# A planned attention and soft-MoE kernel: VectorE's slot-softmax steps in smaller parts inside its wait for the row maxima, value products in pieces of four

## The chip, the cores and the metric

The kernel runs on one core of a Trainium2 chip. The metric is the device time of one execution in microseconds. Three runs of the kernel before took 1103.34, 1103.69 and 1103.90 us, median 1103.69 us.

## The reference

An attention over pooled keys is followed by a soft mixture of experts on its output. The shapes are q (4, 12288, 128), kv (4, 384, 32, 128), 32 slots, 8 experts with 1024 hidden features.

```python
kv_pool = kv.reshape(B, H // r, r, W // r, r, C).mean(axis=(2, 4))      # r = 4: 768 keys per batch
k = v = kv_pool.reshape(B, -1, C) @ w_sr
s = scale * (q @ k.transpose(0, 2, 1))
a = softmax(s, axis=-1)                       # less the row maximum, 1e-09 in the denominator
x = (a @ v).reshape(B * N, C)                 # 49152 rows
logits = x @ phi
d = softmax(logits, axis=0)                   # over all 49152 rows, for each slot
slot_out = experts(d.T @ x)                   # relu(slot @ w1) @ w2, four slots per expert
c = softmax(logits, axis=1)                   # over the 32 slots, for each row
return c @ slot_out
```

## The kernel before

The 49152 query rows are worked on in 96 blocks of 512. A block has six score tiles of 128 keys by 512 rows, two to a PSUM tile (`s0`, `s1`, `s2`, one buffer each). To keep float32 accuracy, q and k are split into a high and a low part, so each score tile is three matmuls (L478 to L480), 18 for a block. Then, for a block:

- VectorE takes the maximum over the keys out of each pair of score tiles (L485, three times), folds the three results (L495) and spreads them for a matmul (L497, tile `rq`). TensorE finishes the maximum across the partitions with one matmul by a selection matrix (L505), and VectorE takes its result up (L510) and turns it into a tile as wide as the block (L515, `mb`). In the text this chain is the row-maximum chain, and L505 is its matmul.
- VectorE subtracts `mb` from the scores in four instructions (L523, two wide and two narrow), which also frees the score tiles for the next block's 18 matmuls.
- ScalarE takes the exponential twice for each half of the block, to float16 (`phi`, L530) and to float32 (`t`, L534); GpSimd subtracts one from the other (`plo`, L539), so that `phi` and `plo` together carry the weights accurately.
- TensorE multiplies the weights by the values, two blocks later. For each of four chunks of 128 rows there are twelve matmuls with `phi` (L556, L557, six key tiles by a high and a low part of the values) and six with `plo` (L564). The result `px` lies in one of two PSUM banks (`m0`, `m1`), two chunks to a bank, and ScalarE copies it to `xl` (L574).

Four blocks make a group. For each group the softmax over rows goes on with a running maximum and a running sum, in steps that the code names 0 to 7: reciprocal of the attention's denominator (0r, L611), logits (1l, GpSimd, L628), their maximum (2, L633 and L635), its spread over the partitions (2q, 2h, 2l, and the matmul 3m, L656), the new running maximum (3, L663, L665, L670), difference, exponential and scaling (4, 5e, 5m: GpSimd L675, ScalarE L684, GpSimd L690), the factor for the old sum (6r, L697; 6s on ScalarE), the slot products (7m, L709, 16 matmuls, in an `m` bank) and the addition to the running sum (7a, L715). Apart from that, L720 takes the row maxima of the logits for the last softmax.

For each batch the keys are pooled and projected, the values get a power-of-two scale out of their largest absolute value (L383 to L409); the largest value is spread over the partitions by a float32 matmul of a diagonal tile `dg` with `ones` (L396). After the last block come the experts and the output stage.

The order of the instructions on each engine is made by a planner (`Plan`), which knows for each operation an engine, a cost, a latency, a due number, and which buffers it takes and frees, and plays the program forward, always taking the operation with the lowest due number among those that can start about now. An operation with `hot=True` (the row-maximum chain) goes first if it can start soon, and a piece of other work is put before it only if it ends in time. The engines then run that order as it stands, waiting for semaphores. The plan's own times set only the order.

Of the kernel before, what the change touches and what calls it, by code (L numbers as in the profile page):

```python
# [32 lines left out]

class Plan:
# [13 lines left out]
    def op(self, eng, cost, lat, prio, deps, fn, acq=(), use=(), at=0.0, slack=0.0, hot=False, raw=0.0):  # L48
# [5 lines left out]
        self.ops.append((eng, cost, lat, prio, list(deps), fn, list(acq), at, slack, hot, raw, list(use)))  # L54
        return n

    def emit(self):
# [115 lines left out]
def attention_then_soft_moe(ctx: ExitStack, tc: tile.TileContext, qT, kv0, kvT, w_sr, w_srT, phi, w1, w2, outT):  # L173
# [456 lines left out]
    def g2(g):  # L630
        d = G[g]
        cm = sm2(g, "cm", [P, TG])[:, : nt(g)]
        nc.vector.tensor_reduce(out=cm, in_=d["L"], axis=X, op=ALU.max, apply_transpose=True)  # L633
# [84 lines left out]
    def k_max(g):  # L718
        o, n = GB[g][0] * TB, nt(g)
        nc.vector.tensor_reduce(out=RM[:, o : o + n], in_=LL[:, o : o + n, :], axis=X, op=ALU.max)  # L720
# [103 lines left out]
    def kv_ops(b, base, step, dep0, dep1):  # L824
# [20 lines left out]
        s = op("PE", 0.6, 0.4, base + step * 5.5, d, lambda: kv_s_mm(b), acq=[("m", ("pa", b))])  # L845
# [10 lines left out]
    def group_ops(g):  # L856
# [398 lines left out]
```

## Time and profile before

| | |
|---|---|
| median of three runs | 1103.69 us (1103.34 to 1103.90) |
| profiled execution, own time | 1102.28 us |
| its span | 1100.5 us (1.8 us lie around it) |
| busy share: TensorE, VectorE, ScalarE, GpSimd | 93%, 89%, 75%, 79% |
| TensorE weight loads | 80% |

A span row of the page's second part has 40 slices of 27.5 us. TensorE stands at 8 or 9 tenths in all but the first and the last few; the tail, about the last 100 us, moves the output. In the timeline a row has its start in us from the span's start, its duration, the engine, the line, the tile written and the tiles read, and how many instructions were merged; in brackets is the idle time before it. Matmuls are pipelined: one begins before the one ahead has ended, so the distance of their starts counts and not their durations.

### The profile page before, as it was taken

Reading aid. Unit: us, or ns where it says so; the run is one execution under the profiler, and the core shown is the slowest. Engines: PE = TensorE matmul, PEld = TensorE weight load, DVE = VectorE, ACT = ScalarE, POOL = GpSimd, SP = SyncE. Lnnn points to the kernel's source line nnn. Section 1 sums busy time; section 2 is a strip of 40 time slices with the busy share of each in tenths; the row PEclk is TensorE's granted clock in tenths of the full one; section 3 lists DMA queues with packets and bytes.
Section 4 is the critical chain, followed back from the end, with each engine's and each line's share of the span. In section 5 each row is a group of like instructions: output and inputs, shape, how many; then the busy total and the mean of one; then the engine's idle time right before and its main releaser. Section 6 shows DMA issues by size and latency. Waiting matters only on the chain.

```text
span 1100.5 us, 24542 instructions
## 1 busy us (share of the span) xinstructions
PE 1028.4 (93%) x10102; PEld 879.2 (80%) x10102; DVE 982.6 (89%) x1494; ACT 826.7 (75%) x1029; POOL 871.8 (79%) x503
## 2 busy tenths in 40 slices
PE   3699999999999999999999999999999999997874
PEld 2588888888888888888888888888888888886342
DVE  7899889899889999899999988989989989997895
ACT  1677778778778878878877788788788777875564
POOL 1579898798899989789899989789889889873341
PEclk9899999999999999999999999999999999999887
DMA  9316401111137300120145310120110110113398
GB/s 345 119 30 146 106 15 40 40 58 40 40 59 154 83 28 13 39 80 19 40 99 114 82 40 2 40 96 2 39 40 2 40 40 1 39 40 116 132 418 368
DMA packets 17406, 89.14 MB, mean 81 GB/s; under 512 B 1680, under 2 KB 3984, under 8 KB 11152
## 3 DMA queue, kind: packets, MB, share of 16 engines
q1 hardware_dynamic: 13408, 69.47, 17.5%
q0 software_dynamic: 3312, 17.70, 8.5%
q8 instruction: 80, 1.31, 0.5%
q10 hardware_dynamic: 576, 0.41, 0.1%
q14 instruction: 30, 0.25, 0.1%
HBM read 58.87 MB, written 25.17 MB: 76 GB/s over the span
## 4 chain that ended last, share of the span: by engine, by line
PE 60%; ACT 18%; DVE 16%; POOL 3%; issue 2%; DMA 1%; SPq 0%; DVEq 0%; ACTq 0%
PE m L564 11%; PE m L556 10%; PE m L557 10%; ACT phi L530 8%; PE s L478 8%; PE s L479 7%; PE s L480 7%; ACT t L534 7%; DVE t L523 4%; DVE r L485 3%; PE m L709 2%; DVE o L1149 2%; PE m L505 2%; POOL plo L539 1%; DVE mb L515 1%
## 5 line engine op out<-in xcount | busy, mean ns | idle before, releaser
L539 POOL TENSOR_TENSOR plo<-t,phi 128x1536 f16<-128x1536 f32 x190 | 594.9, 3136 | 122.1 <-ACT t L534 121.4
L530 ACT ACTIVATE phi<-t,lnk 128x1536 f16<-128x1536 f32 x192 | 301.4, 1570 | 113.8 <-DVE t L523 113.5
L485 DVE TRANSPOSE_TENSOR_REDUCE r<-s 128x32 f32<-128x1024 f32 x288 | 348.7, 1234 | 29.4 <-PE s L480 25.7
L556 PE MATMUL m<-vhi,phi 128*128 128x161 f16 x2280 | 354.7, 234 | 3.0 <-DVE m L510 1.5
L557 PE MATMUL m<-vlo,phi 128*128 128x160 f16 x2280 | 353.8, 233 | 0.0
L523 DVE TENSOR_TENSOR t<-s,mb 128x1024 f32<-128x1024 f32 (+1 forms) x384 | 343.0, 951 | 9.6 <-POOL LL L628 0.5
L534 ACT ACTIVATE t<-t,lnk 128x1536 f32<-128x1536 f32 x192 | 301.6, 1571 | 3.3
L478 PE MATMUL s<-qhi,khi 128*128 128x512 f32 x576 | 239.9, 417 | 6.1 <-DVE t L523 5.8
L556 PEld LDWEIGHTS <-phi 128*128 128x128 f16 x2304 | 224.2, 98 | 23.8 <-issue 23.8
L557 PEld LDWEIGHTS <-phi 128*128 128x128 f16 x2304 | 225.1, 98 | 5.0 <-issue 3.4
L564 PE MATMUL m<-vhi,plo 128*128 128x161 f16 x2280 | 227.7, 234 | 0.4 <-POOL plo L539 0.4
L479 PE MATMUL s<-qlo,khi 128*128 128x512 f32 x576 | 226.8, 394 | 0.0
L480 PE MATMUL s<-qhi,klo 128*128 128x512 f32 x576 | 226.6, 393 | 0.0
L564 PEld LDWEIGHTS <-plo 128*128 128x128 f16 x2304 | 169.9, 98 | 1.2 <-POOL plo L539 0.6
L468 POOL TENSOR_TENSOR qlo<-q,qhi 128x512 fp32r<-128x512 f32 x96 | 128.4, 1338 | 25.4 <-ACT qhi L464 25.4
L574 ACT ACTIVATE xl<-m 128x322 f32<-128x322 f32 x189 | 80.9, 428 | 81.4 <-PE m L564 81.2
L478 PEld LDWEIGHTS s<-qhi,khi 128*128 128x128 f32 x576 | 109.1, 189 | 33.1 <-issue 7.3
L480 PEld LDWEIGHTS s<-qhi,klo 128*128 128x128 f32 x576 | 108.9, 189 | 24.8 <-DVE klo L358 0.5
L479 PEld LDWEIGHTS s<-qlo,khi 128*128 128x128 f32 x576 | 109.4, 190 | 18.7 <-issue 0.7
L515 DVE STREAM_TRANSPOSE mb<-m 128x512 f32<-128x512 f32 x96 | 68.3, 712 | 3.3
L464 ACT ACTIVATE qhi<-q 128x512 fp32r<-128x512 f32 x96 | 59.1, 616 | 1.8 <-DMA q<-qT 1.0
L749 POOL TENSOR_TENSOR LL<-LL,RM 128x512 f32<-128x512 f32 (+2 forms) x25 | 24.8, 1013 | 32.6 <-DVE RM L744 32.6
(146 smaller groups left out, 819.1 us busy)
## 6 DMA issues: line engine op xcount, KB each, us to landing
q<-qT SPq DMA_DIRECT2D x23, 1024.0 KB, 5.0
outT<-o SPq DMA_DIRECT2D x21, 1024.0 KB, 6.3
kva<-kvT POOLq DMA_DIRECT2D x9, 1536.0 KB, 10.8
kva<-kvT SPq DMA_DIRECT2D x3, 1536.0 KB, 10.3
kv<-kv SPq DMA_DIRECT2D x8, 512.0 KB, 5.6
w<-w SPq DMA_DIRECT2D x2, 1536.0 KB, 7.0
w<-w SPq DMA_DIRECT2D x4, 768.0 KB, 4.1
outT<-o SPq DMA_DIRECT2D x6, 512.0 KB, 5.7
```

The lines of the kernel that those rows point to most:

```text
L468: nc.gpsimd.tensor_tensor(out=lo, in0=q_src(i), in1=hi.bitcast(F32), op=ALU.subtract)
L478: nc.tensor.matmul(s, khi[:, ks], hi, start=True, stop=False)
L479: nc.tensor.matmul(s, khi[:, ks], lo, start=False, stop=False)
L480: nc.tensor.matmul(s, klo[:, ks], hi, start=False, stop=True)
L485: nc.vector.tensor_reduce(out=MX[i][:, 2 * u : 2 * u + 2, :].rearrange("p t b -> p (t b)"), in_=S[i, u].rearrange("p t (b j) -> p (t b) j" ...
L523: nc.vector.tensor_tensor(out=TT_[i, h][:, o : o + n, :], in0=S[i, t // 2][:, u : u + n, :], in1=MX[i].unsqueeze(1).broadcast_to([P, n, BQ ...
L530: nc.scalar.activation(hi, TT_[i, h], AF.Exp, bias=lnk, scale=SCALE)
L534: nc.scalar.activation(t, t, AF.Exp, bias=lnk, scale=SCALE)
L539: eng.tensor_tensor(out=lo, in0=TT_.pop((i, h)), in1=PP[i, h], op=ALU.subtract)
L556: nc.tensor.matmul(px, p, vhi[:, t, :], start=(t == 0), stop=False)
L557: nc.tensor.matmul(px[:, 1:], p, vlo[:, t, :], start=False, stop=False)
L564: nc.tensor.matmul(px, PP[i, t // TH][1][:, t % TH, ks], vhi[:, t, :], start=False, stop=(t == NT - 1))
```

## The change

Five things are done, some of them only in the planner's numbers.

1. VectorE's steps of a group are cut smaller: the maximum of the logits (L633) becomes two instructions of half the width, the group's row maxima (L720) four instructions of a quarter, and the running maximum becomes an operation of its own, apart from L663 and L665. The arithmetic is the same.
2. The planner gets a kind of operation called `fill`: until a due time it is taken only where it delays no other operation by more than 0.02 us. VectorE's group steps and the row-maximum quarters are of this kind. And between L497 and L510 VectorE takes only operations that end within 0.55 us of the plan's time.
3. The twelve `phi` products of a chunk, so far one operation of the plan, become three of four matmuls, so that the plan can put other work between them.
4. The tiles `dg` and `ones` become bfloat16, and with them the matmul L396.
5. Costs and latencies in the plan are changed (the row-maximum chain, 0r, 3, 6r, 7a), which moves the order but not the work.

```diff
+AVS = 2
+SPARE = 0.02
...
+            if e in limit:
+                found = [f for f in found if ops[f[2]][9] or f[0] + ops[f[2]][1] <= limit[e]]
...
+            spare = [f for f in found if ops[f[2]][12] is not None and f[0] < ops[f[2]][12]]
+            if spare:
+                rest = [f for f in found if f not in spare]
+                first = min(rest)[0] if rest else inf
+                found = rest + [f for f in spare if f[0] + ops[f[2]][1] <= first + SPARE]
...
-    ones = cp.tile([P, P], F32, tag="ones", name="ones")
+    ones = cp.tile([P, P], BF16, tag="ones", name="ones")
...
-                bp.tile([P, 2, P], F32, tag="dg", name=f"dg_{b}", bufs=1),
+                bp.tile([P, 2, P], BF16, tag="dg", name=f"dg_{b}", bufs=1),
...
-        for t in range(NT):
+        for t in range(t0, t0 + AVS):
...
-        go("2", "DVE", dve(n512) + 0.13, [o["1l"]], g2)
+            go("2a", "DVE", dve(n512 // 2) + 0.06, [o["1l"]], lambda g: g2(g, 0, n16 // 2), fill=True)
+            go("2a", "DVE", dve(n512 // 2) + 0.06, [o["2a"]], lambda g: g2(g, n16 // 2, n16), fill=True)
+        go("2", "DVE", 0.17, [o["2a"]], g2c, fill=True)
...
-        r2 = op("DVE", 0.36, 0.08, T0 + 2, ..., hot=True, raw=0.14)
-        pe = op("PE", 0.16, 0.3, T0 - 10, ..., hot=True)
+        r2 = op("DVE", 0.58, 0.06, T0 + 2, ..., hot=True, raw=0.1, gap=GAP)
+        pe = op("PE", 0.12, 0.12, T0 - 10, ..., hot=True)
...
-            a1 = op("PE", 12 * 0.0705, 0.17, p, ..., lambda i=i, k=k: av_hi(i, k), ...)
+            for t in range(0, NT, AVS):
+                a1 = op("PE", 2 * AVS * 0.0702, 0.17, p, ..., lambda i=i, k=k, t=t: av_hi(i, k, t), ...)
...
-        a = op("DVE", dve(n), 0.08, p, [ops["L", g]] + late, lambda g=g: k_max(g))
+            a = [op("DVE", dve(TB * NS) + 0.05, 0.08, p, [ops["L", g]], lambda g=g, u=u: k_max(g, u), fill=p + 3 * PER) for u in range(GB[g][1])]
```

What this makes of the order is shown at three places. In these rows a line number is that of the kernel which the row is from; the change shifts them (L485 becomes L501, L497 L513, L505 L521, L510 L526, L556 and L557 L572 and L573, L564 L580, L709 L732, L720 L745).

First place: VectorE, the maxima of block 35, ahead of which (before) the logits' maximum `cm` of a group stands. Before, ahead of the row maxima `r` and inside the wait between `rq` and the next `m`:

```order
L633 TENSOR_REDUCE cm_4994<-LL 128x16
L635 TENSOR_REDUCE cmt_4996<-cm_4994 128x1
L485 TENSOR_REDUCE r_35_5002<-s_0_4978 128x32
L485 TENSOR_REDUCE r_35_5002<-s_1_4989 128x32
L485 TENSOR_REDUCE r_35_5002<-s_2_5005 128x32
L495 TENSOR_REDUCE m_116<-r_35_5002 128x16
L497 TENSOR_TENSOR rq_5054<-m_116,quad 128x64
L720 TENSOR_REDUCE RM<-LL 128x16
L510 TENSOR_REDUCE m_35_5070<-m_116 128x16
```

Now:

```order
L501 TENSOR_REDUCE r_35_5022<-s_0_5005 128x32
L650 TENSOR_REDUCE cm_5032<-LL 128x8
L501 TENSOR_REDUCE r_35_5022<-s_1_5016 128x32
L650 TENSOR_REDUCE cm_5032<-LL 128x8
L501 TENSOR_REDUCE r_35_5022<-s_2_5028 128x32
L655 TENSOR_REDUCE cmt_5074<-cm_5032 128x1
L511 TENSOR_REDUCE m_117<-r_35_5022 128x16
L513 TENSOR_TENSOR rq_5081<-m_117,quad 128x64
L745 TENSOR_REDUCE RM<-LL 128x4
L526 TENSOR_REDUCE m_35_5095<-m_117 128x16
```

The two halves of `cm` stand between the row maxima, `cmt` behind them, and a quarter of the group's row maxima in the wait, where the whole stood.

Second place: VectorE, block 33, where the factor `al` and the running sum `acc` stand, before and now:

```order
L697 TENSOR_REDUCE al_4713<-da_4567 128x1
L485 TENSOR_REDUCE r_33_4724<-s_0_4689 128x32
L715 TENSOR_TENSOR acc<-acc,m_116 128x129
L485 TENSOR_REDUCE r_33_4724<-s_1_4720 128x32
L485 TENSOR_REDUCE r_33_4724<-s_2_4733 128x32
L495 TENSOR_REDUCE m_116<-r_33_4724 128x16
```

```order
L501 TENSOR_REDUCE r_33_4730<-s_0_4713 128x32
L501 TENSOR_REDUCE r_33_4730<-s_1_4725 128x32
L720 TENSOR_REDUCE al_4765<-da_4654 128x1
L501 TENSOR_REDUCE r_33_4730<-s_2_4737 128x32
L745 TENSOR_REDUCE RM<-LL 128x4 x2
L738 TENSOR_TENSOR acc<-acc,m_117 128x129
L511 TENSOR_REDUCE m_117<-r_33_4730 128x16
```

The factor and the sum have moved behind the second and the third row maximum, with two quarters of the group's row maxima ahead of the sum.

Third place: TensorE in the same block, around the 16 slot products, before (behind the first of the six score tiles) and now (behind the last):

```order
L478 MATMUL s_0_4689<-qhi_4495,khi_2405 128x512
L479 MATMUL s_0_4689<-qlo_4496,khi_2405 128x512
L480 MATMUL s_0_4689<-qhi_4495,klo_2406 128x512
L709 MATMUL m_116<-xl_3802,D_4565 32x129 x16
L478 MATMUL s_0_4689<-qhi_4495,khi_2405 128x512
```

```order
L494 MATMUL s_2_4737<-qhi_4478,khi_2387 128x512
L495 MATMUL s_2_4737<-qlo_4479,khi_2387 128x512
L496 MATMUL s_2_4737<-qhi_4478,klo_2388 128x512
L732 MATMUL m_117<-xl_3812,D_4652 32x129 x16
L572 LDWEIGHTS phi_0_4575
```

The slot products now lie between the score tiles and the value products that lead to the row-maximum matmul. That matmul itself, 30 products later, stands between eight and four `phi` products of a chunk, where it stood behind all twelve.

More of the change, by code (lines that the diff above doesn't have):

```diff
@@ L46, in __init__, with op @@
         self.bank = 0
-    def op(self, eng, cost, lat, prio, deps, fn, acq=(), use=(), at=0.0, slack=0.0, hot=False, raw=0.0):
+    def op(self, eng, cost, lat, prio, deps, fn, acq=(), use=(), at=0.0, slack=0.0, hot=False, raw=0.0, fill=None, gap=0.0):
         n = len(self.ops)
@@ L53, in op @@
             self.users.setdefault(key, []).append(n)
-        self.ops.append((eng, cost, lat, prio, list(deps), fn, list(acq), at, slack, hot, raw, list(use)))
+        self.ops.append((eng, cost, lat, prio, list(deps), fn, list(acq), at, slack, hot, raw, list(use), fill, gap))
         return n
@@ L143, in emit @@
             free[e] = t + cost
+            if ops[n][13] > 0:
+                limit[e] = t + cost + ops[n][13]
+            elif ops[n][13] < 0:
+                limit.pop(e, None)
             end = done[n] = t + cost + lat
@@ L292, in attention_then_soft_moe @@
     SL = 0.5
+    LATE = 6.0
+    GAP = 0.55
     def kv_load(plan_):
@@ L715, in g7a, with k_max @@
         nc.vector.tensor_tensor(out=acc, in0=acc, in1=G[g]["pd"][:, : C + 1], op=ALU.add)
-    def k_max(g):
+    def k_max(g, u=None):
         o, n = GB[g][0] * TB, nt(g)
+        if u is not None:
+            o, n = o + u * TB, TB
         nc.vector.tensor_reduce(out=RM[:, o : o + n], in_=LL[:, o : o + n, :], axis=X, op=ALU.max)
@@ L844, in kv_ops @@
         d = [op("ACT", 0.4, 0.1, base + step * 5, m[0] + m[1], lambda k=k: kv_d(b, k)) for k in range(2)]
[L845 removed]
+        s = op("PE", 0.25, 0.4, base + step * 5.5, d, lambda: kv_s_mm(b), acq=[("m", ("pa", b))])
         s = op("DVE", 1.1, 0.08, base + step * 5.5, [s], lambda: kv_s_g(b), use=[("m", ("pa", b))])
@@ L882, in group_ops, with go @@
         k = [0]
-        def go(name, eng, cost, dep, f, acq=(), use=(), path=None):
+        def go(name, eng, cost, dep, f, acq=(), use=(), path=None, fill=False):
             k[0] += 1
-            o[name] = op(eng, cost, 0.08, base + step * k[0], dep, lambda: f(g), acq=list(acq), use=[xl] + list(use) if name in ("0", "1v", "1l", "7m") else list(use), slack=0.0 if fast else SL, raw=0.14)
+            due = base + step * k[0] + LATE if fill and not fast else None
+            o[name] = op(eng, cost, 0.08, base + step * k[0], dep, lambda: f(g), acq=list(acq), use=[xl] + list(use) if name in ("0", "1v", "1l", "7m") else list(use), slack=0.0 if fast else SL, raw=0.14, fill=due)
         go("0", small, sm_(1), deps, g0)
-        go("0r", "DVE", 0.18, [o["0"]], g0r)
+        go("0r", "DVE", 0.21, [o["0"]], g0r, fill=True)
         go("1u", small, sm_(1), [o["0r"]], g1u)
@@ L900, in group_ops @@
         go("3m", "PE", 0.25 if fast else 0.12, [o["2q"]], g3m, acq=[mc])
-        go("3", "DVE", 0.45, [o["3m"]] + ([ops["g3", g - 1]] if g else []), g3, use=[mc])
+        go("3c", "DVE", 0.42, [o["3m"]], g3, use=[mc], fill=True)
+        go("3", "DVE", 0.19, [o["3c"]] + ([ops["g3", g - 1]] if g else []), g3r, use=[mc], fill=True)
         ops["g3", g] = o["3"]
@@ L907, in group_ops @@
         if g:
-            go("6r", "DVE", 0.1, [o["5m"]], g6r)
+            go("6r", "DVE", 0.18, [o["5m"]], g6r, fill=True)
             go("6s", small, 0.3, [o["6r"]] + prev, g6s)
@@ L911, in group_ops @@
         go("7m", "PE", 0.07 * n16, [o["5m"], o["1v"]], g7m, acq=[md], use=[("D", g)])
-        go("7a", "DVE", 0.21, [o["7m"]] + prev, g7a, use=[md])
+        go("7a", "DVE", 0.25, [o["7m"]] + prev, g7a, use=[md], fill=True)
         ops["g7", g] = o["7a"]
@@ L1025, in attention_then_soft_moe @@
         late = [] if g < FAST - 1 else end_ + [last[LG, "g"]]
-        a = op("DVE", dve(n), 0.08, p, [ops["L", g]] + late, lambda g=g: k_max(g))
-        a = op("POOL", 1.05 * n / 512, 0.1, p, [a, ops["g4", g]], lambda g=g: k_sub(g))
+        if late:
+            a = [op("DVE", dve(n), 0.08, p, [ops["L", g]] + late, lambda g=g: k_max(g))]
+        else:
+            a = [op("DVE", dve(TB * NS) + 0.05, 0.08, p, [ops["L", g]], lambda g=g, u=u: k_max(g, u), fill=p + 3 * PER) for u in range(GB[g][1])]
+        a = op("POOL", 1.05 * n / 512, 0.1, p, a + [ops["g4", g]], lambda g=g: k_sub(g))
         ops["ke", g] = op("ACT", act(n), 0.1, p, [a], lambda g=g: k_exp(g))
```

34 lines of the change are left out of this document (22 added, 12 removed).

## The prediction

> **What bounds the kernel now.** I read the page's busy shares first, then the windows, the list of waits, and the timeline of one group of four blocks.
>
> ```profile
> PE 1028.4 (93%) x10102; PEld 879.2 (80%) x10102; DVE 982.6 (89%) x1494; ACT 826.7 (75%) x1029; POOL 871.8 (79%) x503
> ...
> 130.53:170.52 39.99, 39.45 (x399) 34.64 (x399) 36.53 (x53) 31.69 (x39) 35.53 (x21) 1.00 0.22 55
> 571.50:611.50 40.00, 39.44 (x402) 34.65 (x400) 36.54 (x54) 31.67 (x38) 36.90 (x22) 1.00 0.56 116
> ...
> DVE m L510 <- PE m L505: 30.3, 71, 0.5
> DVE r L485 <- PE s L480: 25.7, 33, 1.0
> PE m L505 <- ACT t L534: 6.6, 14, 0.8
> PEld m L505 <- ACT t L534: 10.2, 17, 1.0
> ```
>
> TensorE is busy 93% of the span and 98.6% of a 40 us stretch in the middle, at the full granted clock (1.00); VectorE is busy 91% there, ScalarE 79%, GpSimd 89%. So two engines are nearly full, and each is seen waiting for the other: VectorE 30.3 us for the row-maximum matmul L505, TensorE 16.8 us ahead of that same matmul. (The list names ScalarE for the latter; `rq`, the input of L505, is VectorE's, and the rows below show L505 starting 0.14 us after `rq`.) What can be gained without taking work off TensorE is its idle time, and that is small. Two stretches 441 us apart have the same length, so one group can stand for the rest. It runs from one L505 to the fourth after it:
>
> ```profile
> 354.93 0.27 PE L505 MATMUL m<-rq,sel_r 128*128 128x64 f32 x1
> 358.01 0.47 PE L478 MATMUL s<-qhi,khi 128*128 128x512 f32 x1
> 358.88 1.09 PE L709 MATMUL m<-xl,D 128*32 128x129 f32 x32
> 359.90 0.50 PE L478 MATMUL s<-qhi,khi 128*128 128x512 f32 x1
> 363.48 0.24 PE L556 MATMUL m<-vhi,phi 128*128 128x161 f16 x1
> 365.61 0.30 PE L505 MATMUL m<-rq,sel_r 128*128 128x64 f32 x1
> 368.72 0.47 PE L478 MATMUL s<-qhi,khi 128*128 128x512 f32 x1
> 372.93 0.24 PE L556 MATMUL m<-vhi,phi 128*128 128x161 f16 x1
> 375.14 0.27 PE L505 MATMUL m<-rq,sel_r 128*128 128x64 f32 x1
> 383.72 0.23 PE L556 MATMUL m<-vhi,phi 128*128 128x161 f16 x1
> 384.48 0.23 PE L557 MATMUL m<-vlo,phi 128*128 128x160 f16 x1
> 385.15 0.27 PE L505 MATMUL m<-rq,sel_r 128*128 128x64 f32 x1 [0.44 <-ACT t L534]
> 394.95 0.27 PE L505 MATMUL m<-rq,sel_r 128*128 128x64 f32 x1
> ```
>
> The four intervals are 10.68 ("sum", with the 16 slot products L709), 9.53 ("reciprocal"), 10.01 ("maximum") and 9.80 us ("new maximum"), together 40.02. TensorE's pieces can be read off: from L505 to the score tiles 3.08 (6, 12, 6, 12, 6 value products), the 18 score matmuls 4.21 (368.72 to 372.93), then 12, 6 and 12 value products 2.13 (363.48 to 365.61, where L505 follows at once), twelve of them 0.84 (383.72 to 384.48 and one more). In the maximum interval it idles 0.6 us: twelve products end at 384.55, L505 starts at 385.15.
>
> VectorE in the same group:
>
> ```profile
> 359.78 0.18 DVE L697 TENSOR_REDUCE al<-da 128x1 f32<-128x32 f32 x1
> 360.92 1.25 DVE L485 TRANSPOSE_TENSOR_REDUCE r<-s 128x32 f32<-128x1024 f32 x1 [0.96 <-PE s L480]
> 365.94 0.23 DVE L510 TENSOR_REDUCE m<-m 128x16 f32<-128x64 f32 x1 [0.39 <-PE m L505]
> 367.02 3.55 DVE L523 TENSOR_TENSOR t<-s,mb 128x1024 f32<-128x1024 f32 x4
> 370.48 2.53 DVE L485 TRANSPOSE_TENSOR_REDUCE r<-s 128x32 f32<-128x1024 f32 x2
> 372.94 0.21 DVE L611 RECIPROCAL r<-xl 128x16 f32<-128x16 f32 x1
> 373.12 1.25 DVE L485 TRANSPOSE_TENSOR_REDUCE r<-s 128x32 f32<-128x1024 f32 x1
> 374.40 0.33 DVE L495 TENSOR_REDUCE m<-r 128x16 f32<-128x96 f32 x1
> 374.77 0.23 DVE L497 TENSOR_TENSOR rq<-m,quad 128x64 fp32r<-128x64 f32 x1
> 379.99 0.70 DVE L633 TRANSPOSE_TENSOR_REDUCE cm<-LL 128x16 f32<-128x512 f32 x1
> 387.72 0.15 DVE L663 TENSOR_REDUCE c<-m 128x1 f32<-128x4 f32 x1
> 388.17 0.19 DVE L670 TENSOR_TENSOR mrun<-mrun,m 128x32 f32<-128x32 f32 x1
> 390.61 3.50 DVE L485 TRANSPOSE_TENSOR_REDUCE r<-s 128x32 f32<-128x1024 f32 x3
> ```
>
> The reciprocal interval shows the loop. The last row maximum starts 0.19 after the score tiles end (372.93 to 373.12), `rq` is ready 1.88 later (375.00), L505 follows 0.14 after that, so L505 comes 2.02 after the last row maximum starts; TensorE, with 2.13 of products to do, is ready 0.09 sooner. Reckoned from an L505, the first row maximum can start at 4.87 (365.61 to 370.48), and each takes 1.16 more (three in 3.50, each overlapping the next by 0.08). In the maximum and new-maximum intervals VectorE's group steps make the row maxima late, and TensorE waits 0.6 and 0.3 (the pieces are 9.42 of the 9.80, and step 3m's two small matmuls); in the sum interval TensorE is late by the slot products, and VectorE waits 0.96.
>
> **The change part by part**, by the new order, as distances from the L505 that opens the interval.
>
> *Maximum interval.* Ahead of the row maxima nothing stands now; two halves of L633 stand between them.
>
> ```profile
> L633 DVE TRANSPOSE_TENSOR_REDUCE cm<-LL x25: 311/702/703, 96.7 to 1011.9; 128x16 f32<-128x512 f32 x23, 128x12 f32<-128x384 f32 x1, 128x4 f32<-128x128 f32 x1
> L720 DVE TENSOR_REDUCE RM<-LL x25: 266/675/686, 100.5 to 1017.4; 128x16 f32<-128x512 f32 x23, 128x12 f32<-128x384 f32 x1, 128x4 f32<-128x128 f32 x1
> L675 POOL TENSOR_TENSOR D<-LL,mrun x23: 1273/1302/1750, 106.3 to 992.8; 128x512 f32<-128x512 f32 x23
> L690 POOL TENSOR_TENSOR D<-D,rv x23: 1042/1048/1065, 110.7 to 997.3; 128x512 f32<-128x512 f32 x23
> L539 POOL TENSOR_TENSOR plo<-t,phi x190: 3099/3118/3577, 39.0 to 994.2; 128x1536 f16<-128x1536 f32 x190
> ...
> 358.17 1.58 ACT L530 ACTIVATE phi<-t,lnk 128x1536 f16<-128x1536 f32 x1 [1.53 <-DVE t L523]
> ...
> L396 PE MATMUL m<-dg,ones x8: 378/379/483, 29.2 to 739.6; 128*128 128x256 f32 x8
> ```
>
> Between 0.311 at 128 elements and 0.702 at 512, a half (256) comes to 0.44, 0.36 net of the overlap. The last row maximum starts at 4.87 + 2 x (1.16 + 0.36) = 7.91, L505 at 9.94 with 2.03. TensorE has six more products ahead of L505 (0.43): 3.08 + 4.21 + 2.13 + 0.43 = 9.85. I take 9.95 (9.85 to 10.1, the upper end if the small L635 behind the third maximum isn't hidden): 0.06 gained, and the six products no longer stand behind L505.
>
> *New-maximum interval.* L663, L665, L670 leave the middle of the subtractions and go between the row maxima: 0.34 (387.72 to 388.14 less the overlap) and 0.11. Last maximum 4.87 + 1.16 + 0.34 + 1.16 + 0.11 = 7.64, L505 at 9.67. TensorE, now 2.66 from its score tiles, has to wait for the first subtraction (1.23 of the 3.55, ending at 2.6) and is ready at 2.7 + 4.21 + 2.13 = 9.1, so it idles about 0.5. Gain 0.13. The quarter of L720 that stands in this interval's and the next one's wait (0.27 by the 0.266 at 128 elements) fits into 0.39, where the whole (0.675) did not.
>
> *Sum interval.* TensorE: 3.08, score tiles 4.21, slot products 1.02 and 0.1 for the switch, then 0.85 + 0.44 and eight products 0.56: 10.26, against 10.68. Of the 0.42, 0.28 are the four products that now follow L505, 0.14 the second switch inside the score tiles. VectorE, with the last maximum at 7.29 + 0.19 = 7.48, two quarters (0.19 each net), the sum 0.21 and L495 to L497 in 0.60, has `rq` at 9.8 and waits: 0.3 of cover. ScalarE's part of the sum now stands behind three exponentials of 1.58 (the first, at 358.17, starts 3.2 after L505), a copy of `px` and one of q, so done at about 9.0: not late.
>
> *Reciprocal interval.* The four products come first: score tiles end at 3.38 + 4.21 = 7.59, L505 at 7.59 + 0.19 + 2.02 = 9.80, 0.27 longer than before.
>
> Sum: 10.26 + 9.80 + 9.95 + 9.67 = 39.68, that is 0.34 less per group. The order has this pattern in 18 of 22 groups. In three, all twelve products and six more stand between the slot products and L505: 10.97 + 9.38 (the score tiles start at 2.7 there) + 9.95 + 9.67 = 39.97, 0.05 less. Six of the 18 hold a batch's key and value work, which TensorE does anyway; I count half for them. So 12 x 0.34 + 6 x 0.17 + 3 x 0.05 = 5.3 us.
>
> *L396 in bfloat16*: four uses, three in the loop, each with two records of 0.38. A bfloat16 matmul of this width is not in the trace: between nothing and 0.7 saved each. I take the middle, 1.0 us for three. *Start and tail*: the first seven blocks keep their order; in the tail the last groups' steps shuffle, and TensorE's slot products of the last full group go behind more value products. Bounds -2 to +2, taken as 0. DMA issues stay in their order on SP; GpSimd's keep their number.
>
> Together -6.3 us: the profiled execution's 1102.28 becomes 1096.0, and against the median, 1.4 higher, 1103.7 becomes 1097.4.
>
> [...] The rows give 0.675 - 4/3 x (0.675 - 0.266) = 0.13 fixed, and 0.08 of that overlaps the neighbour.
>
> **The rivals.**
>
> *All of TensorE's waits go.* The finer pieces let L505 follow `rq` at once everywhere, and other products fill the wait. About 0.97 a group (0.6 + 0.28 + 0.09) times 21 and the 1.0: 22 us, 1082. Against it: in the new-maximum interval the chain is VectorE's, 9.67 by its own rows.
>
> *The waits only move.* TensorE has 39.0 of the 40 us filled; 0.1 more on VectorE in three intervals eats 0.3 of the 0.34, and with the 1.0 of L396 it is 1102. What speaks for it is that two of the intervals get only 0.06 and 0.13.
>
> *The cut costs what it adds.* If each of the four added instructions pays its fixed 0.13 in full on the loop, 0.52 a group, the 0.34 is overdrawn by 0.18: 21 times that less 1.0 is +2.8, 1106.5. Against it: three of the four stand in the wait or under TensorE's 0.3 of cover. [...]
>
> *GpSimd holds the slot products* (slower). The new running maximum now ends at 7.7 of its interval instead of 3.2, behind which GpSimd subtracts (L675, 1.30, after a `plo` of 3.12 that starts behind two exponentials, near 6.8, and ends near 9.9), ScalarE exponentiates, GpSimd does another `plo` and multiplies (L690, 1.05). By these the multiplied tile is there at about 6 of the sum interval, and the slot products, now at 7.4, have 1.4 to spare (before, they stood at 3.95). If one more `plo` gets ahead, 3.12, TensorE waits 1.7 in each of 21 groups: +36 - 6, 1133. It decides the sign from 1.7 us of delay on.
>
> **How the numbers follow.** Likeliest, 0.55: 1097.4, own range 1093 to 1101. All waits go 0.11; waits move 0.19; the cut costs 0.06; GpSimd 0.09. A difference under 0.2% (2.2 us) is about what a measurement here can't tell from none. Faster 0.66, same 0.19, slower 0.15. The range 1088 to 1106 takes in the likeliest, the waits that move and the parts of the others next to them, and leaves out 2 in 10.
>
> **What would show it.** In the profile after: a group of about 39.7 us; VectorE's 0.96 wait behind L697 gone; waits of L510 on L505 fewer than 71, by the 21 more that hold a quarter; TensorE idle 0.4 to 0.6 ahead of L505 in the new-maximum interval alone; the sum interval at 10.3, the reciprocal one at 9.8. I am wrong if the slot products wait for GpSimd, if the maximum interval stays above 10.0, or if the tail moves by over 2 us.

## The result, and the profile after

The kernel after takes 1093.59 us (median of five runs, 1093.21 to 1094.81) where the kernel before takes 1103.69: a ratio of 0.9914, 95% interval 0.9899 to 0.9928. That is 10.1 us less, where 6.3 were forecast. The profiled execution took 1093.54 us, its span 1091.8, so 8.7 less than the profiled span before.

Line 3 of the page after, busy time and share by engine:

```profile
PE 1026.5 (94%) x10098; PEld 883.1 (81%) x10098; DVE 988.0 (90%) x1583; ACT 823.3 (75%) x1029; POOL 870.9 (80%) x503
```

Its list of waits (who waits for whom: us in all, times, longest), the rows on the row-maximum chain:

```profile
DVE m L526 <- PE m L521: 36.5, 90, 0.9
...
PEld m L521 <- DVE rq L513: 6.4, 5, 2.6
...
PE m L572 <- DVE m L526: 5.4, 17, 0.3
...
DVE r L501 <- PE s L496: 4.6, 11, 0.9
...
PE m L521 <- DVE rq L513: 3.5, 5, 2.0
...
PE m L521 <- ACT cq L606: 0.5, 2, 0.3
```

and of the list before, the row for the same matmul that stands beside the 6.6 us shown in the prediction:

```profile
PE m L505 <- DVE rq L497: 4.4, 10, 2.0
```

VectorE's wait for the score tiles has gone from 25.7 to 4.6 us. A PE and a PEld row of the row-maximum matmul show largely the same waits: in the profile before the weight load at 385.12 us follows 0.61 of waiting, its matmul at 385.15 follows 0.44. So only one of the two is to be counted. By the PE rows TensorE waited 11.0 us ahead of this matmul before (6.6 and 4.4, in 24 places) and 4.0 now (3.5 and 0.5, in 7). Another wait has grown to 5.4 us in 17 places: value products L572 that wait for L526, behind the matmul.

The windows of the four intervals of one group after, from L521 to L521, in the order sum, reciprocal, maximum, new maximum (columns: length, then busy time and count of PE, PEld, DVE, ACT, POOL, granted clock, DMA share, GB/s):

```profile
353.24:363.45 10.21, 10.21 (x122) 9.01 (x120) 9.45 (x16) 8.53 (x11) 10.21 (x8) 1.00 0.52 107
363.45:373.20 9.75, 9.75 (x99) 8.74 (x97) 8.89 (x12) 7.18 (x9) 9.32 (x6) 1.00 0.33 79
373.20:383.04 9.84, 9.84 (x99) 8.90 (x98) 9.31 (x15) 8.62 (x12) 8.54 (x5) 1.00 0.52 112
383.04:392.66 9.62, 9.30 (x91) 8.04 (x88) 9.12 (x16) 7.28 (x10) 8.22 (x5) 1.00 0.22 41
```

The group takes 39.42 us, 0.60 less than the 40.02 of before. TensorE is busy all the time in three of the intervals; only the new-maximum interval holds idle time, 0.32 us.

The timeline of VectorE in the maximum interval shows the new places:

```profile
378.05 1.24 DVE L501 TRANSPOSE_TENSOR_REDUCE r<-s 128x32 f32<-128x1024 f32 x1
379.21 0.40 DVE L650 TRANSPOSE_TENSOR_REDUCE cm<-LL 128x8 f32<-128x256 f32 x1
379.54 1.21 DVE L501 TRANSPOSE_TENSOR_REDUCE r<-s 128x32 f32<-128x1024 f32 x1
380.67 0.40 DVE L650 TRANSPOSE_TENSOR_REDUCE cm<-LL 128x8 f32<-128x256 f32 x1
381.00 1.21 DVE L501 TRANSPOSE_TENSOR_REDUCE r<-s 128x32 f32<-128x1024 f32 x1
...
382.67 0.22 DVE L513 TENSOR_TENSOR rq<-m,quad 128x64 fp32r<-128x64 f32 x1
382.81 0.28 DVE L745 TENSOR_REDUCE RM<-LL 128x4 f32<-128x128 f32 x1
383.35 0.22 DVE L526 TENSOR_REDUCE m<-m 128x16 f32<-128x64 f32 x1 [0.26 <-PE m L521]
```

A half of `cm` takes 0.40, and the next maximum starts 0.33 after the half does. The quarter of the row maxima stands in the wait behind `rq` and leaves 0.26 of it. TensorE at the same place:

```profile
383.04 0.27 PE L521 MATMUL m<-rq,sel_r 128*128 128x64 f32 x1
383.63 0.23 PE L572 MATMUL m<-vhi,phi 128*128 128x161 f16 x1 [0.32 <-DVE m L526]
```

L521 doesn't wait, but the products behind it begin 0.59 later, where in the run with the old costs below they follow in 0.11: they open the next pair of chunks in the `m` bank in which L521's result lies, and wait 0.32 of it for L526, which reads that result.

Where the 8.7 us between the two profiles come from (by the starts of the row-maximum matmuls; a group is four blocks):

| stretch | before | after | change | forecast |
|---|---|---|---|---|
| start, to block 8 | 110.34 | 111.79 | +1.45 | 0 |
| twelve plain groups | | | -6.7 | -4.1 |
| six groups with key and value work, L396 with them | | | -3.3 | -2.0 |
| three groups with all products ahead of L505 | | | -0.1 | -0.15 |
| blocks 92 to 95 | 30.59 | 29.92 | -0.7 | |
| tail, from block 95 | 107.77 | 108.36 | +0.6 | 0 |

### The profile page after: what moved, and what is told of

Its sections match the earlier page's. It is cut to its first block, busy times and chain, and to the rows that moved or that the text cites. A ratio compares the mean times of both kernels' runs of the same rounds, so it can differ in the third digit from the quotient of the medians.

```text
span 1091.8 us, 24577 instructions
## 1 busy us (share of the span) xinstructions
PE 1026.5 (94%) x10098; PEld 883.1 (81%) x10098; DVE 988.0 (90%) x1583; ACT 823.3 (75%) x1029; POOL 870.9 (80%) x503
## 4 chain that ended last, share of the span: by engine, by line
PE 84%; DVE 7%; ACT 6%; issue 2%; DMA 0%; POOL 0%; SPq 0%; DVEq 0%; ACTq 0%
PE m L572 14%; PE m L580 14%; PE m L573 13%; PE s L494 12%; PE s L496 11%; PE s L495 11%; PE m L732 2%; ACT phi L546 2%; ACT t L550 2%; PE po L1177 2%; DVE o L1186 2%; PE m L521 1%; DVE pool L332 1%; DVE t L539 1%; DVE r L501 1%
## 5 line engine op out<-in xcount | busy, mean ns | idle before, releaser
L501 DVE TRANSPOSE_TENSOR_REDUCE r<-s 128x32 f32<-128x1024 f32 x288 | 355.6, 1238 | 12.2 <-PE s L496 4.6
L572 PE MATMUL m<-vhi,phi 128*128 128x161 f16 x2280 | 356.3, 234 | 8.7 <-DVE m L526 5.4
L573 PE MATMUL m<-vlo,phi 128*128 128x160 f16 x2280 | 355.5, 233 | 0.0
L572 PEld LDWEIGHTS <-phi 128*128 128x128 f16 x2304 | 223.9, 98 | 23.3 <-issue 23.3
L573 PEld LDWEIGHTS <-phi 128*128 128x128 f16 x2304 | 225.2, 98 | 10.8 <-issue 10.6
L580 PE MATMUL m<-vhi,plo 128*128 128x161 f16 x2280 | 227.1, 234 | 0.0
L580 PEld LDWEIGHTS <-plo 128*128 128x128 f16 x2304 | 173.0, 98 | 0.6 <-issue 0.6
L495 PEld LDWEIGHTS s<-qlo,khi 128*128 128x128 f32 x576 | 110.2, 191 | 19.7 <-issue 0.7
L531 DVE STREAM_TRANSPOSE mb<-m 128x512 f32<-128x512 f32 x96 | 68.3, 711 | 3.3
L526 DVE TENSOR_REDUCE m<-m 128x16 f32<-128x64 f32 x96 | 21.5, 224 | 36.5 <-PE m L521 36.5
```

The lines of the kernel that those rows point to most:

```text
L495: nc.tensor.matmul(s, khi[:, ks], lo, start=False, stop=False)
L501: nc.vector.tensor_reduce(out=MX[i][:, 2 * u : 2 * u + 2, :].rearrange("p t b -> p (t b)"), in_=S[i, u].rearrange("p t (b j) -> p (t b) j" ...
L572: nc.tensor.matmul(px, p, vhi[:, t, :], start=(t == 0), stop=False)
L573: nc.tensor.matmul(px[:, 1:], p, vlo[:, t, :], start=False, stop=False)
L580: nc.tensor.matmul(px, PP[i, t // TH][1][:, t % TH, ks], vhi[:, t, :], start=False, stop=(t == NT - 1))
```

## The experiments

**Theory 1**: the gain comes from where the group steps stand on VectorE and the slot products on TensorE. Its rivals were the finer pieces, the cutting by itself, and one engine as the only bound. All kernels are timed against the kernel before on the same chip, and interval lengths are of the group that starts at block 32.

**The pieces of value products made whole again, in the kernel after.**

```diff
-AVS = 2
+AVS = 6
```

> The kernel after, with the twelve phi products of a chunk as one piece again; all else stays, VectorE's order too but for a few places. In a group of the order the products that stood behind the row-maximum matmul of the sum interval (four) go ahead of it again: by the pieces, sum 10.21 + 0.28 = about 10.5, reciprocal 9.75 - 0.25 = 9.5, the other two as after. Theory 1 (the gain comes from where the group steps stand on VectorE and the slot products on TensorE; the finer pieces only shift 0.28 from one interval to the next): group 39.5, total about 1095 (1093 to 1097). Rival (the finer pieces carry the gain, since the planner can fill TensorE's waits with them): the group goes back towards 40.0, total 1101 to 1104.

Measured: 1096.41 us, ratio 0.9933 [0.9920, 0.9945]. The windows:

```profile
353.03:363.54 10.51, 10.51 (x127) 9.29 (x124) 9.46 (x16) 8.72 (x11) 10.26 (x9) 1.00 0.52 108
363.54:373.05 9.51, 9.51 (x94) 8.48 (x92) 8.81 (x12) 6.77 (x8) 9.07 (x5) 1.00 0.33 85
373.05:382.90 9.85, 9.85 (x99) 8.90 (x98) 9.31 (x15) 8.75 (x12) 8.79 (x6) 1.00 0.49 107
382.90:392.52 9.62, 9.31 (x90) 8.03 (x87) 9.12 (x16) 7.27 (x10) 8.21 (x5) 1.00 0.22 41
```

The sum interval is 0.30 longer and the reciprocal one 0.24 shorter: the four products went from one to the other, and this plain group loses 0.07. The pieces are worth more in the groups where key and value work stands: the first of each pair takes 42.9 with whole chunks, 42.05 with pieces, 2.5 us in the three, of which the second ones give back 0.4. One plain group, from block 28, takes 40.58 instead of 39.41, another 1.2 us. The totals of the two kernels are hard to tell apart; from block 8 to block 92 the profile has 845.15 us instead of 841.70.

**The pieces alone, in the kernel before.** The same cut of the twelve products, and nothing else.

> The kernel before with the twelve phi products as three pieces of four in the plan, and nothing else of the change. In the order the pieces of a chunk still stand together in nearly every block, and the group's pattern is that of before. Theory (pieces alone move nothing): 1103.7 (1102 to 1105). Rival (TensorE's 0.97 of waits in a group is filled with pieces): 1090 to 1098.

Measured: 1103.64 us, ratio 0.9999 [0.9991, 1.0008]. Alone they are worth nothing; what they gain, they gain in the new order.

**The instructions of L633 and L720 whole again, in the kernel after.**

```diff
-go("2a", "DVE", dve(n512 // 2) + 0.06, ..., lambda g: g2(g, 0, n16 // 2), fill=True)
-go("2a", "DVE", dve(n512 // 2) + 0.06, ..., lambda g: g2(g, n16 // 2, n16), fill=True)
+go("2a", "DVE", dve(n512) + 0.09, ..., lambda g: g2(g, 0, n16), fill=True)
+k[0] += 1
...
-a = [op("DVE", dve(TB * NS) + 0.05, ..., lambda g=g, u=u: k_max(g, u), ...) for u in range(GB[g][1])]
+a = [op("DVE", dve(n), ..., lambda g=g: k_max(g), ...)]
```

> The kernel after, with L633's and L720's instructions whole again (cm in one piece of 0.70, the group's row maxima in one piece of 0.675), everything else kept, the due numbers of the later steps too. In the order the whole cm stands behind the first row maximum, and the whole row maxima ahead of the running sum in the sum interval, none in the wait of the row-maximum chain. Theory 1: the places matter more than the cut; maximum interval 9.93 (one fixed part less, but cmt not fully hidden), new maximum 9.62, sum 10.5 (the twelve products stand whole ahead of the row-maximum matmul, VectorE at about 10.1 to 10.3), reciprocal 9.5: group 39.6, total about 1097 (1095 to 1099). Rival (the cutting itself is the gain, because a quarter fits into the wait and a whole does not): the whole piece's 0.6 lies on the loop again, group 39.9 to 40.0, total 1102 to 1104.

Measured: 1097.39 us, ratio 0.9947 [0.9933, 0.9960], intervals 10.48, 9.51, 9.86 and 9.79, together 39.64. Most of the gain is there without the cut of these two: 0.38 of the 0.60. The kernel after is 0.22 a group better, but 0.17 of that lies in the new-maximum interval and doesn't come from VectorE. The products behind L521 wait longer here, 0.49 for ScalarE's copy of the `px` before them, where it was 0.32 for L526; the new pair takes the bank that is being copied:

```profile
384.44 0.23 PE L572 MATMUL m<-vhi,phi 128*128 128x161 f16 x1 [0.49 <-ACT xl L590]
```

So about 0.05 a group is left for the cut itself in this run.

**Twelve of the sixteen slot products left out, in the kernel after.**

```diff
-for k in range(n):
+for k in range(n if g >= FAST else NQD):
```

> The kernel after with only 4 of the 16 slot products of every full group (twelve left out, so the slot sums lack three quarters of the rows; nothing else changes, order as after). It takes 12 x 0.064 = 0.77 us off TensorE in each sum interval. Theory 1 (VectorE's chain is right behind TensorE there: its rq is done 0.28 ahead of the row-maximum matmul): the sum interval falls by 0.25 only, 10.21 to about 9.95, total 1088 (1086 to 1090). Rival (TensorE alone sets the loop after the change, at 94% busy): 0.77 x 22 = 17 us less, 1077.

Measured: 1086.72 us, ratio 0.9845 [0.9832, 0.9859]. The windows of the sum and the maximum interval, and of TensorE the slot products and the matmul that ends the sum interval:

```profile
351.14:361.14 10.00, 9.78 (x99) 8.35 (x96) 9.46 (x16) 8.32 (x11) 10.00 (x8) 1.00 0.53 108
...
370.91:380.76 9.85, 9.85 (x100) 8.91 (x98) 9.31 (x15) 8.62 (x12) 8.66 (x6) 1.00 0.51 111
```

```profile
358.55 0.43 PE L732 MATMUL m<-xl,D 128*32 128x129 f32 x8
358.91 0.24 PE L572 MATMUL m<-vhi,phi 128*128 128x161 f16 x1
...
361.14 0.30 PE L521 MATMUL m<-rq,sel_r 128*128 128x64 f32 x1 [0.22 <-DVE rq L513]
```

From the first slot product to the next value product it is 0.36 us here and 1.02 in the kernel after (360.63 to 361.65), so 0.66 of TensorE's work is gone (0.77 had been expected). That shortens the interval by 0.21, and then L521 waits for `rq`. So VectorE's chain stands 0.2 behind TensorE's there: TensorE at 94% is not the only bound.

**Every quarter of the row maxima done twice, in the kernel after.**

```diff
+nc.vector.tensor_reduce(out=RM[:, o : o + n], in_=LL[:, o : o + n, :], axis=X, op=ALU.max)
 nc.vector.tensor_reduce(out=RM[:, o : o + n], in_=LL[:, o : o + n, :], axis=X, op=ALU.max)
```

> The kernel after with every quarter of the group's row maxima done twice (same data, same result), four more VectorE instructions of 0.27 in a group, order otherwise as after. Of the four quarters one or two stand in the wait of the row-maximum chain (0.26 of it left beside the first quarter) and two in the sum interval (VectorE 0.28 ahead of TensorE). Theory 1 (the quarters stand where VectorE has cover): 0 to 0.1 in the waits, 0.1 in the sum interval, 0.1 to 0.2 a group, total 1096 (1094 to 1098). Rival (VectorE, 90% busy, is the bound and each instruction costs its fixed part and length on the loop): four times 0.19 to 0.27 a group, 16 to 23 us, 1110 to 1117.

Measured: 1097.83 us, ratio 0.9951 [0.9939, 0.9964]; intervals 10.68, 9.77, 9.84 and 9.61. The timeline of VectorE in the wait that opens the new-maximum interval, two quarters in it (L746 is the doubled one):

```profile
383.56 0.28 DVE L745 TENSOR_REDUCE RM<-LL 128x4 f32<-128x128 f32 x1
383.87 0.29 DVE L746 TENSOR_REDUCE RM<-LL 128x4 f32<-128x128 f32 x1
384.10 0.23 DVE L526 TENSOR_REDUCE m<-m 128x16 f32<-128x64 f32 x1
```

A second quarter in this wait costs nothing: L526 starts 0.31 after the matmul L521, as in the kernel after, and 9.61 is that kernel's length. In the wait that opens the sum interval it makes L526 0.05 later (0.38 after L521 instead of 0.33). The 0.47 lies in the sum interval: these 0.05, and 0.65 for two more quarters between the row maxima and `acc`, of which 0.2 is covered. That lies between the 0.1 to 0.2 expected and the 0.76 to 1.08 of the rival (four times 0.19 to 0.27): the two quarters in the waits cost 0.05 together, the two others what the cover doesn't take. What an instruction costs here is decided by its place.

**Theory 2** came out of the plan's text. A step's due number is `base + step * k`, and `k` counts the steps of the group; `step` is 0.85 x 9.8 x 4 / 20 = 1.67 us. The cut adds two steps at 2 and one at 3, so that everything behind them is due 3.3 to 5 us later. This isn't in the list of the change, and it might be what moved the order.

**The later due numbers alone, in the kernel before.**

```diff
+k[0] += 0 if fast else 3
 go("2", "DVE", dve(n512) + 0.13, [o["1l"]], g2)
```

> The kernel before with one edit of the plan's numbers: from step 2 on, every step of a group is due three steps later (3 x 1.67 us, what the three added steps of the change do to the due numbers of those behind them). Nothing is cut, no cost is changed. By itself this moves the order most of the way: the whole cm stands behind the first row maximum, the new maximum between the second and the third, the slot products behind the score tiles; the whole of L720 stays in the wait. Theory 2 (the due numbers make part of the gain, the cut the rest): maximum 9.93, new maximum 9.85, sum 9.7, reciprocal 10.35 (twelve products behind the row-maximum matmul come first): group 39.85, total 1100 (1098 to 1102). Rival 1 (the due numbers are all of it): 1094 to 1096. Rival 2 (the cut is all of it): 1103.7.

Measured: 1104.35 us, ratio 1.0005 [0.9996, 1.0014]. Its windows (before: 10.68, 9.53, 10.01, 9.80):

```profile
354.56:364.48 9.92, 9.88 (x112) 8.45 (x112) 9.06 (x13) 8.08 (x11) 9.92 (x7) 1.00 0.48 98
364.48:374.82 10.34, 10.34 (x104) 9.31 (x104) 8.90 (x12) 8.53 (x12) 9.77 (x7) 1.00 0.37 97
374.82:384.83 10.01, 9.58 (x94) 8.48 (x92) 9.39 (x14) 7.85 (x11) 9.17 (x6) 1.00 0.63 125
384.83:394.62 9.79, 9.79 (x93) 8.40 (x93) 9.42 (x15) 7.37 (x8) 7.45 (x5) 1.00 0.00 1
```

The reciprocal interval came as expected (10.34), two others didn't: 9.92 for 9.7, since VectorE's sum, late now, waits for ScalarE's part of it,

```profile
363.51 0.29 DVE L715 TENSOR_TENSOR acc<-acc,m 128x129 f32<-128x129 f32 x1 [0.19 <-ACT acc L590]
```

and 10.01 for 9.93 in the maximum interval, where the whole `cm` stands between the maxima. Nothing gained: what the slot products' new place saves in one interval, the twelve products behind L505 add to the next.

The run with the two instructions whole had these due numbers too, and gained 0.38. The traces show two differences of place between the two. There the twelve products stood ahead of the row-maximum matmul (its sum and reciprocal intervals take 19.99 together, here 20.26), and the small `cmt` stood one row maximum behind `cm`, where here it follows at once: from `cm` over `cmt` to the next maximum it is 0.79 here, against 0.59 and 0.05 there, and the maximum interval takes 10.01 against 9.86.

**The cut with the old due numbers.** The kernel after, where the three added steps don't count.

```diff
+k[0] -= 1
 go("2a", "DVE", ..., lambda g: g2(g, n16 // 2, n16), fill=True)
+k[0] -= 0 if fast else 1
 go("2", "DVE", 0.17, [o["2a"]], g2c, fill=True)
...
+k[0] -= 0 if fast else 1
 go("3", "DVE", 0.19, ...)
```

> The kernel after with the due numbers of the steps of a group put back to what they were (the three added steps don't count), so cut, pieces, costs and rules are all there. In the order the two intervals with the maxima look as after, but the slot products stand ahead of the last score tile in most groups, with all twelve products and six more ahead of the row-maximum matmul. Theory 2 (the later due numbers, which take the slot products behind the score tiles, are needed): maximum 9.84, new maximum 9.62, sum 3.08 + 4.21 + 1.2 + 2.13 + 0.43 = 11.05, reciprocal 9.5 to 9.65: group 40.0 to 40.15, total 1102 (1100 to 1105), the gain gone. Rival (the cut gives the gain by itself): 1094 to 1096.

Measured: 1106.76 us, ratio 1.0029 [1.0020, 1.0039]: slower than before.

```profile
355.22:366.28 11.06, 11.06 (x132) 9.64 (x130) 9.57 (x16) 8.81 (x11) 11.06 (x9) 1.00 0.45 93
366.28:375.93 9.65, 9.20 (x88) 8.10 (x87) 8.91 (x12) 6.62 (x8) 7.76 (x5) 1.00 0.43 107
375.93:385.77 9.84, 9.84 (x99) 8.90 (x98) 9.31 (x15) 8.91 (x12) 9.35 (x6) 1.00 0.62 124
385.77:395.35 9.58, 9.26 (x90) 8.03 (x87) 9.11 (x16) 7.23 (x10) 8.13 (x5) 1.00 0.01 2
```

All four lengths are the expected ones. The two intervals with the maxima keep their gain (0.39), and the sum interval takes it back and more, because the slot products stand ahead of the last score tile and VectorE waits for that tile again:

```profile
363.96 1.25 DVE L501 TRANSPOSE_TENSOR_REDUCE r<-s 128x32 f32<-128x1024 f32 x1 [0.88 <-PE s L496]
```

The total came 1.8 above the upper end of what was expected; the plain group did not, so that part lies in the other groups and the tail.

So everything but the later due numbers gains nothing, and the later due numbers in the kernel before gain nothing. Together they gain, and mostly without the cut of L633 and L720. What is needed beside the due numbers isn't taken apart by these runs: the rule for `fill`, the limit in the wait, the running maximum as an operation of its own and the other costs were never left out one by one.

**The old costs of the row-maximum chain, in the kernel after.**

```diff
-r2 = op("DVE", 0.58, 0.06, T0 + 2, ..., raw=0.1, gap=GAP)
-pe = op("PE", 0.12, 0.12, T0 - 10, ...)
+r2 = op("DVE", 0.36, 0.08, T0 + 2, ..., raw=0.14, gap=GAP)
+pe = op("PE", 0.16, 0.3, T0 - 10, ...)
```

(and likewise for L526, L531 and the subtractions).

> The kernel after with the old costs of the row-maximum chain in the plan. In the order the maximum interval loses the six products ahead of its row-maximum matmul, and the new-maximum interval begins with these six, so that no pair of products is opened right behind that matmul; two quarters stand in waits. It tells whether TensorE's 0.47 us behind the row-maximum matmul (the pair that waits for L526) is a cost of its own. Theory 1 (both intervals are VectorE's, 9.84 and 9.62; TensorE's idle time only changes its place, to ahead of the row-maximum matmul): group 39.4, total 1094 (1092 to 1096). Rival (the wait for the bank is what the group pays for): 0.4 a group less, 1085 to 1087.

Measured: 1091.08 us, ratio 0.9883 [0.9870, 0.9897]. The windows of the maximum and the new-maximum interval, and the matmul between them:

```profile
371.49:381.33 9.84, 9.58 (x92) 8.46 (x92) 9.31 (x16) 8.61 (x12) 8.56 (x5) 1.00 0.50 107
381.33:390.88 9.55, 9.55 (x94) 8.42 (x94) 9.27 (x17) 7.43 (x10) 8.13 (x5) 1.00 0.23 41
```

```profile
381.33 0.27 PE L521 MATMUL m<-rq,sel_r 128*128 128x64 f32 x1 [0.27 <-DVE rq L513]
```

The group is 39.38, as in the kernel after: the idle time that stood behind L521 now stands ahead of it, and the six products have gone from the maximum into the new-maximum interval. The maximum interval has its 9.84 with TensorE idle for 0.26, so VectorE's chain sets it. The new-maximum interval falls by 0.07; TensorE is busy all the time in it, so both engines are near their limit there. At most 0.07 of that wait for L526 was a cost of its own, not 0.4. The 2.5 us come from elsewhere, which the next pair of runs shows.

**The same again, beside the kernel after.**

> The kernel after, unchanged, beside the next one for a direct comparison: 1093.6 (1092.5 to 1095).

> The kernel after with the old costs of the row-maximum chain in the plan once more, beside the kernel after. Theory: the plain group is the same (39.4), but the three groups in which slot products, twelve products and six more stood ahead of the row-maximum matmul (40.0 to 40.2) come down to 39.4 to 39.6, 1.5 together, and the groups with key and value work by 0.2: 1091 (1090 to 1092.5), below the kernel after. Rival (the difference is that of two runs): 1093.6.

Measured: the kernel after 1093.75 us, ratio 0.9919 [0.9904, 0.9935]; with the old costs 1089.37 us, ratio 0.9874 [0.9861, 0.9886]. The intervals don't meet: of the kernels that do the whole work this is the fastest. From block 8 to 92 the two profiles differ by 2.1 us. The three groups of the other pattern take 39.65, 39.43 and 39.42 instead of 40.10, 40.02 and 40.00 (1.6 us), the second groups of the key and value pairs 0.5 less in all, and the last group 0.3 more. Another 1.2 lie in the tail, where two profiles of one program differ by up to 0.5. So the new costs of the row-maximum chain, a part of point 5 of the change, lose about 2 us in the loop; the cause inside the three groups wasn't followed further.

**One half of `cm` and the quarters only in the wait.** The kernel after, with one more rule.

```diff
 if e in limit:
     found = [f for f in found if ops[f[2]][9] or f[0] + ops[f[2]][1] <= limit[e]]
+else:
+    found = [f for f in found if not ops[f[2]][14] or f[0] >= ops[f[2]][12] + XTRA]
```

> The kernel after with one more rule in the plan: the second half of cm and the quarters of the row maxima are taken on VectorE only in the wait between rq and the next m (unless they are 20 us late). In the order of some third to half of the groups one half of cm leaves the maximum interval for the wait, the new maximum goes into the sum interval's subtractions and the slot products into the reciprocal interval. Theory 1 (VectorE's chain sets the maximum and new-maximum intervals, what is put into the wait costs nothing): these fall to 9.6 and 9.45 in such groups, the other two take 9.75 and 10.3: group 39.1 there, 39.4 in the others, total 1091 (1088 to 1095). Rival (TensorE is full, and what VectorE saves only shifts the idle time): 1093 to 1095, or more where the rearranged slot products stand badly, up to 1098.

Measured: 1097.29 us, ratio 0.9941 [0.9929, 0.9954], slower than the kernel after (845.62 us from block 8 to block 92, where that has 841.70). The windows of a group with the new order, from the maximum interval on:

```profile
373.29:382.87 9.58, 9.58 (x93) 8.47 (x92) 9.04 (x14) 7.32 (x9) 8.71 (x5) 1.00 0.45 110
382.87:392.45 9.58, 9.58 (x92) 8.48 (x92) 9.13 (x15) 7.34 (x9) 7.52 (x4) 1.00 0.07 13
392.45:402.16 9.71, 9.71 (x94) 8.55 (x94) 9.33 (x17) 8.03 (x11) 9.37 (x8) 1.00 0.23 42
402.16:412.78 10.62, 10.62 (x123) 9.26 (x124) 9.37 (x16) 9.31 (x14) 10.62 (x8) 1.00 0.23 69
```

The maximum interval falls by 0.26 as theory 1 has it. But every later step of the group comes a block later, the slot products meet a full interval (10.62, expected 10.3), and the group is 39.49, nothing gained; groups in which the two orders meet take 40.2 to 41.0. TensorE is busy through all four intervals: the rival, that TensorE is full and badly placed slot products cost time, has it right.

**L412 in float32 again, in the kernel after.** The tiles `dg` and `ones` as before, every other row of the order in its place.

> The kernel after with dg and ones (L412) in float32 again; the order is otherwise the same, row for row. It tells what the bfloat16 matmul is worth: before, each use had two records of 0.38, after, one of 0.28; three uses lie in the loop. Theory (TensorE is full there, the difference lies on the path): 1.0 to 1.5 more, 1095. Rival (it stands in idle time of the kv blocks): 1093.6.

Measured: 1094.34 us, ratio 0.9916 [0.9903, 0.9929], which can't be told from the kernel after. The profiles can tell. The windows of the first group that holds the matmul, in the kernel after and here:

```profile
232.78:273.66 40.88, 39.83 (x409) 35.21 (x406) 37.90 (x65) 34.85 (x45) 36.15 (x23) 1.00 0.08 27
```

```profile
231.70:272.93 41.23, 40.23 (x409) 35.42 (x407) 38.00 (x65) 34.86 (x45) 36.13 (x23) 1.00 0.08 28
```

0.35 there, 0.35 and 0.32 in the two other groups that hold it, and within 0.07 in all the rest: 1.0 us in the loop.

## Why the prediction was right, and where its sizes were off

*The direction and the mechanism* held: the time fell into the likeliest case's own range (1093 to 1101), at its lower end, because the steps of VectorE went out of the way of the row maxima and the slot products behind the score tiles. Most of the gains were put too small. In the profiles the loop gained 10.8 us, and the start and the tail took 2.0 back, most of it by chance; so the 8.7 lie closer to the forecast than the loop does. The twelve plain groups hold most of the miss, 6.7 us where 4.1 were counted; the groups with key and value work 1.3, and blocks 92 to 95, which the sum leaves out, 0.7.

*The maximum interval*, 9.95 forecast, 9.84 measured, is the interval most off. The row maxima start 1.49 and 1.46 apart where 1.52 was reckoned, and the first 4.85 after L521 instead of 4.87. A half of `cm` was put at 0.44, between 0.311 and 0.702; it took 0.40, 0.33 net of the overlap instead of 0.36, twice. The second maximum took 1.13 net instead of 1.16, which the three in 3.50 had shown already (1.24 each, so 0.11 of overlap and not 0.08). L635 is hidden: L521 comes 2.04 after the last maximum, with 2.03 reckoned.

*The new-maximum interval*, 9.67 forecast, 9.62 measured, is right partly by luck. The last maximum starts 7.69 after L521 instead of 7.64, held up by its score tile (which ends at 390.69; the maximum starts at 390.73), and the next L521 follows 1.93 behind it instead of 2.03: two differences that nearly cancel. So TensorE stands closer to VectorE here than the prediction had it. The idle time of 0.5 on TensorE is there, but ahead of the row-maximum matmul, where the prediction put it, there is none: 0.48 stand behind the one that opens the interval. The experiment with the old costs moves 0.26 to its front and shows that the group loses next to nothing by it. In the kernel L521's result lies in columns 448 to 511 of the bank and `px` in columns 0 to 321, so the products don't overwrite it; they wait all the same. The row at 383.63 shows the wait, 0.32 for L526; its reason isn't shown, and no run here leaves it out.

*The sum and the reciprocal interval*, 10.26 and 9.80 forecast, 10.21 and 9.75 measured. VectorE's cover in the first, put at 0.3, was measured twice: 0.2 by leaving out slot products and by doubling the quarters.

*The three groups of the other pattern*: -0.05 each forecast, -0.04 measured.

*The six groups with key and value work*, "I count half for them", is a guess without a row behind it, and was too small: -2.0 with L396 forecast, -3.3 measured, of which 1.0 is L396, as forecast (the middle of its bounds, so that is luck). The rest, 2.3, is 0.38 a group where 0.17 was counted, and the run with whole chunks shows that the pieces of products bring nearly all of it in the new order (2.2).

*Start and tail at nothing*: +1.45 and +0.6 in this profile. Most of the start is chance, since a second profile of the same program reaches block 8 at 110.92 instead of 111.79 (before: 110.34). For the tail 0.6 is about as much as two profiles of one program differ in it (108.36 and 108.87).

*TensorE's 16.8 us* ahead of L505 were misread: they add a PE and a PEld row that show the same waits; it waited 11.0. No term of the sum hangs on it.

*Fewer waits of L510, by 21*, was wrong: 90 instead of 71. Before, the whole of L720 (0.675) overfilled the wait (0.39 to 0.45 where L720 isn't in it); a quarter (0.27) leaves 0.20 to 0.26 of it, so the row stays, and the waits without L720 stay too.

*The rivals.* The slot products don't wait for GpSimd: TensorE is busy for all 10.21 us of the sum interval. That the cut costs what it adds is settled by the doubled quarters: the fixed part is paid (two halves of `cm` take 0.80 us where the whole took 0.70, four quarters of the row maxima 1.10 where the whole took 0.675, so 0.10 and 0.14 for each added instruction), but in a wait a whole added quarter costs 0.05 or nothing. That the waits only move describes TensorE in the new-maximum interval alone (0.3 ahead of L505 before, 0.48 behind L521 now), and even there 0.18 was gained. TensorE's waits didn't all go: 39.10 of 39.42 are filled.

*What the prediction did not see*: it took the new order as it stood and didn't ask which of the five points made it. The due numbers had moved with the number of steps, which the list of the five doesn't name, and without that the same cut makes the kernel slower than before. And it has no term for the new costs of the row-maximum chain by themselves, which lose about 2 us in the loop.

## What to carry to other kernels

When a step of a planned kernel is cut in two, look at what counts the steps: here the due numbers behind the cut moved by up to 5 us, without which there was no gain, while most of the gain stayed when two of the instructions were made whole again. An instruction that is added to a nearly full engine (VectorE at 90% here) is priced by its place: two more quarters in the waits cost 0.05 us a group, two more in the sum interval 0.42. Look for the wait it stands in and how much of it is left, and for how far the engine is ahead of the other one there. Where two engines set a loop in turn, work taken off one in one interval is worth only the distance to the other's chain (0.66 us less on TensorE shortened the sum interval by 0.21), and an idle gap that another order moves to the other side of the same instruction, at nearly the same length of the group (39.42 and 39.38), was hardly a cost of its own.

## What the runs showed of the hardware

The loop repeats far better than the whole run. From block 8 to block 92 two profiles of the kernel after, taken at different times, took 841.70 and 841.76 us, two of the version with the old costs 839.53 and 839.63. Over all kernels here the stretch up to block 8 spread from 110.0 to 112.0 and the tail, whose order differs between them, from 107.7 to 110.2. Up to block 4 the granted clock was 0.93 in the profile before, 0.88 in the one after, and 0.93 again in the second profile of the kernel after:

```profile
0.00:71.66 71.66, 44.30 (x289) 35.58 (x289) 59.97 (x91) 34.60 (x37) 31.45 (x20) 0.93 0.48 178
```

```profile
0.00:73.30 73.30, 46.09 (x288) 37.41 (x288) 60.06 (x91) 34.70 (x37) 30.14 (x20) 0.88 0.47 174
```

```profile
0.00:72.44 72.44, 44.93 (x287) 36.19 (x288) 59.94 (x91) 34.69 (x37) 31.19 (x20) 0.93 0.47 176
```

For one and the same program (the last two rows) TensorE's busy time there differs by 1.2 us and the stretch by 0.9; that the clock is the cause of the longer start isn't shown. An effect of a microsecond, such as that of L412 (1.0 in the loop), is read from the groups and not from the total.
